# A convolution by transforms: real and imaginary parts on the two partition halves, and one full-height product per frequency

## The chip, the cores and the metric

The kernel runs on one core of a Trainium2 chip. The metric is device time in microseconds (us), the median of several runs. The core's engines are TensorE (PE in the profile; its weight loads are listed apart as PEld), VectorE (DVE), ScalarE (ACT), GpSimd (POOL) and SyncE (SP, which here only issues DMAs).

## What is computed

```python
def _attn_ref(x, h):                       # x (8, 5696, 128), h (5696, 128)
    B, S, D = x.shape
    L = 2 * S
    Xf = np.fft.rfft(x, n=L, axis=1)
    Hf = np.fft.rfft(h, n=L, axis=0)
    y = np.fft.irfft(Xf * Hf[None], n=L, axis=1)[:, :S, :]
    return y

def _moe_ref(x, w_theta, w_tok_r, w_tok_i, w_ch):
    theta = x @ w_theta
    zr, zi = x * np.cos(theta), x * np.sin(theta)
    y = np.einsum('ts,bsd->btd', w_tok_r, zr) + np.einsum('ts,bsd->btd', w_tok_i, zi)
    u = x + y
    return u + np.maximum(u @ w_ch, 0.0)
```

The second function gets what the first returns. The first is a long convolution over the sequence for every batch and channel; the second mixes tokens with two 5696 x 5696 matrices. The change lies wholly in the first.

## The kernel before

**The convolution** is done by transforms that are split in two factors: 5696 = 89 x 64 (N1 = NB = 89, N2 = 64), with K1 = 90 frequencies in the first factor. The work goes in eight groups. A group (L129) is two batch entries (called e = 0 and 1) and one half of the channels (HD = 64, called d). The transform of h is made once, ahead of the groups, by the same code. A group passes through these stages:

- **Stage A** (L245 to L263), 16 chunks of four d. For one d, the weights are x at [89 rows, 2 x 64 columns] (both batch entries, L477) and what streams is the table f1_t, 180 columns: 90 cosines and 90 sines. So one product (L255) puts 128 rows (e, n) and 180 columns (real and imaginary part, frequency) into PSUM. A chunk's four products are taken to the tile `a` by one copy of 128x720, on ACT (L262) or on DVE (L260).
- **f2** (L270 to L282), 12 chunks of up to eight frequencies. The tile `a` has the batch entry on its partition halves (64 rows each). For one frequency there are four products (L278) of 64 rows: two batch entries, and for each the real part and the imaginary part, which are added up in PSUM. The table `w_t2` holds 3 x 64 columns a frequency, so that a window of 128 columns gives either of the two; its lower and upper partitions hold the same frequencies, 45 slots apart (`slot`, L186). A chunk is copied to `xs` by ACT (L404, 128x1024), in the order e, d, frequency. For h, ACT takes batch entry 0's place (L332) and DVE the other (L333).
- **Products** with the transform of h, two for each chunk (L408, DVE).
- **Stage C** (L429, 16 chunks of 16 products) and **stage D** (L453, 7 chunks), with copies on ACT (L435, L459) or DVE (L433, L457).

All PSUM tiles of these stages come from one pool of four, each two banks wide (L100, L103).

**The order** is written out by hand. ACT and DVE (and, up to L507, POOL) keep program order. The string `PLAN` (L511) gives, for one group, the order of the chunks of stage C and D of a group (c, d), of stage A of the next one (a) and of its f2 and products (f, p, q, r); a capital letter puts the copy on DVE. `PLAN_0` is that of the first group, in which the e tables are made as well (t). When stage A of a group is through, POOL issues the loads of x for the next but one (L139), since x has a single buffer; they are 16 DMAs a group.

**The tables** are made at the start. For `w_t2`, three blocks of 15 slots: POOL writes indices (`index`, L157), DVE turns them into turns (`w_turns`, L191), ACT rounds them (L192), DVE takes the part below one and its absolute value (`w_angles`, L164 and L167), ACT takes the sines (`w_sines`, L170 and L173). `w_rest` (L205) completes a block on DVE: the odd half by a factor (L209), the negative third (L210), and two copies across the partition halves (L212) into the other 45 slots. The copy of h to its tile (L297) stands behind `w_rest(0)` on DVE; `w_rest(1)` and `w_rest(2)` stand ahead of and behind stage A of h. On POOL the first loads of x (L139, from L292) follow the indices.

**The token mixing** comes after all groups, from some 420 us on: products of 128x512 (L1299, L1387), whose weights are loaded by POOL's DMAs and transposed by DVE. One row of tiles in it (L1263) uses weights of 64 columns and writes the two halves of the PSUM partitions in turn.

Of the kernel before, what the change touches and what calls it, by code (L numbers as in the profile page):

```python
# [23 lines left out]
def kernel(  # L24
# [10 lines left out]
    nc = tc.nc  # L35
# [96 lines left out]
    def load_x(g):  # L132
# [11 lines left out]
    in_order = ExitStack()  # L144
    in_order.enter_context(tc.manual_schedule(engines={
        mybir.EngineType.DVE, mybir.EngineType.Activation, mybir.EngineType.Pool}))
    lane = fc.tile([P, 7], F32)
    for p0 in (0, 64):
        nc.gpsimd.iota(lane[p0:p0 + 64, 0:1], pattern=[[0, 1]], base=0, channel_multiplier=1,
                       allow_small_or_imprecise_dtypes=True)  # L150
    nc.gpsimd.iota(lane[:, 1:2], pattern=[[0, 1]], base=0, channel_multiplier=1,
                   allow_small_or_imprecise_dtypes=True)
    nc.vector.memset(lane[0:64, 2:3], QUARTER)
    nc.vector.memset(lane[64:P, 2:3], QUARTER + KH)

    def index(k, pattern, base):
        nc.gpsimd.iota(k, pattern=pattern, base=base, channel_multiplier=0,  # L157
                       allow_small_or_imprecise_dtypes=True)
# [10 lines left out]
    def sine(out_, r, sign):  # L169
        nc.scalar.activation(out_, r, AF.Sin, bias=zero_b[:r.shape[0]], scale=-sign * TWO_PI)  # L170

    def cosine(out_, k):
        nc.scalar.activation(out_, k, AF.Sin, bias=half_pi[:k.shape[0]], scale=-TWO_PI)  # L173

    w_t2 = keep.tile([P, K1, 3 * N2], F16, tag="keep", name="w_t2")
    assert WB + BT + 3 * P * 2 <= K1 * 3 * N2
    f1_t = fc.tile([P, 2 * K1], F16)
    odd = lane[:, 4:5]
    WS = 15
    WQ = WS * 32  # L180
    w_all = s1.tile([P, 2 * KH // WS * WQ], F32, name="w_all")
    w_of = [tuple(w_all[:, (2 * b + n) * WQ:(2 * b + n + 1) * WQ] for n in range(2)) for b in range(KH // WS)]
# [3 lines left out]
    def slot(e, k1):  # L186
        return (k1 + e * KH) % K1

    def w_turns(b):
        t, k = w_of[b]  # L190
        nc.vector.tensor_scalar(t, k, lane[:, 2:3], lane[:, 3:4], op0=add, op1=mult)  # L191
        nc.scalar.activation(k, t, AF.Identity, bias=magic)  # L192

    def w_angles(b):
        t, k = w_of[b]
        below_one(t, k)
        absolute(k, t)

    def w_sines(b):
        t3, k3 = (z.rearrange("p (k n) -> p k n", n=32) for z in w_of[b])  # L200
        here = w_t2[:, WS * b:WS * b + WS]
        sine(here[:, :, :32], t3, 1)
        cosine(here[:, :, N2:N2 + 32], k3)

    def w_rest(b):  # L205
        s0 = WS * b
        here = w_t2[:, s0:s0 + WS]
        two = here[:, :, :2 * N2].rearrange("p k (f a n) -> p k f a n", f=2, a=2)
        nc.vector.tensor_scalar(two[:, :, :, 1], two[:, :, :, 0], odd, None, op0=mult)  # L209
        nc.vector.tensor_scalar(here[:, :, 2 * N2:], here[:, :, :N2], -1.0, None, op0=mult)  # L210
        for p0 in (0, 64):
            nc.vector.tensor_copy(w_t2[p0:p0 + 64, KH + s0:KH + s0 + WS],  # L212
                                  w_t2[64 - p0:P - p0, s0:s0 + WS])

    nc.scalar.activation(f1_t[:, :1], zero_b, AF.Sin, bias=zero_b)
    for b in range(len(w_of)):
        index(w_of[b][1], [[1, WS], [N1, 32]], WS * b)
        if b == 0:
            index(f_k, [[1, K1]], 0)
# [5 lines left out]
    below_one(o_t, o_k)  # L225
    absolute(o_k, o_t)
    nc.vector.tensor_scalar(odd, o_k, -4.0, 1.0, op0=mult, op1=add)
    w_turns(0)
    nc.vector.tensor_scalar(f_t, f_k, QUARTER, lane[:NB, 5:6], op0=add, op1=mult)
    up(f_t, f_k)  # L230
    below_one(f_t, f_k)
    absolute(f_k, f_t)
    w_turns(1)
    w_angles(0)
    w_sines(0)
    sine(f1_t[:NB, K1:], f_t, -1)
    cosine(f1_t[:NB, :K1], f_k)
    w_turns(2)
    w_angles(1)
    w_sines(1)  # L240
    w_angles(2)
    w_sines(2)
    w_rest(0)

    def stage_a(lhs):  # L245

        st = {}

        def chunk(n, on_dve=False):
            q = 4 * n  # L250
            if q == 0:
                st["a"] = fa.tile([P, 2 * K1, HD], F16, tag="a", name="a_")
            ps = psum()
            for i in range(4):
                nc.tensor.matmul(ps[:, i // 2, (i % 2) * 2 * K1:(i % 2 + 1) * 2 * K1], lhs(q + i), f1_t[:NB],  # L255
                                 start=True, stop=True)
            a_out = st["a"][:, :, q:q + 4].rearrange("p k (a q) -> p k a q", a=2)
            a_in = ps[:, :, :4 * K1].rearrange("p a (q k) -> p k a q", q=2)
            if on_dve:
                nc.vector.tensor_copy(a_out, a_in)  # L260
            else:
                nc.scalar.activation(a_out, a_in, AF.Copy)  # L262
        return chunk, st  # L263

    def steps_of(chunk, count, on_dve=()):
        return [lambda n=n: chunk(n, n in on_dve) for n in range(count)]
# [3 lines left out]
    def f2(a_st, c):  # L270

        c0, ck = CHK[c]
        ps = psum()
        for j in range(ck):
            for ri in range(2):
                for e in range(2):
                    rows = slice(64 * e, 64 * e + 64)
                    nc.tensor.matmul(ps[:, e, j * HD:(j + 1) * HD],  # L278
                                     w_t2[rows, slot(e, c0 + j), N2 * (1 - ri):N2 * (3 - ri)],
                                     a_st["a"][rows, ri * K1 + c0 + j, :],  # L280
                                     start=(ri == 0), stop=(ri == 1))
        return ps[:, :, :ck * HD].rearrange("p e (k d) -> p e d k", k=ck)  # L282

    def woven(*lists):

# [13 lines left out]
    h_chunk_a, a_h = stage_a(lambda q: h16[:NB].rearrange("p h n d -> p (h n) d")[:, :, q])  # L299
    w_rest(1)  # L300
    for f in steps_of(h_chunk_a, NA, (4, 6, 8, 10, 12, 14)):
        f()
    w_rest(2)

    for t in uv_t:
        nc.gpsimd.memset(t[:, :, UVW:], 0.0)
# [15 lines left out]
    def h_part(c):  # L322
        return h_flat(c).rearrange("p (r d k) -> p r d k", r=2, k=CHK[c][1])
# [5 lines left out]
    def h_chunk(c):  # L329
        c0, ck = CHK[c]  # L330
        ps = f2(a_h, c)
        nc.scalar.activation(h_part(c)[:, 0], ps[:, 0], AF.Copy, scale=8.0 / S)  # L332
        nc.vector.tensor_scalar(h_later[:, HD * c0:HD * (c0 + ck)].rearrange("p (d k) -> p d k", k=ck),  # L333
                                ps[:, 1], 8.0 / S, None, op0=mult)

    def h_other(c, n):
        own = halves(hs_of[c][0], c, n, hs_of[c][1])
# [60 lines left out]
    def stage_b(a_st, refill):  # L398
        xs_of, made = {}, [0] * NCK

        def spectrum(c):
            ps = f2(a_st, c)
            xs = xs_of[c] = fs.tile([P, 2, HD, CK], F16, tag="xs", name="xs")
            nc.scalar.activation(xs[:, :, :, :CHK[c][1]], ps, AF.Copy)  # L404

        def products(c, e):
            c0, ck = CHK[c]
            nc.vector.tensor_tensor(  # L408
                uv[e][:, :, :, c0:c0 + ck],
                xs_of[c][:, e:e + 1, :, :ck].to_broadcast([P, 2, HD, ck]), h_part(c), op=mult)  # L410
# [62 lines left out]

    def front(g):
        dh = groups[g][1]
        x16 = x16s[g].rearrange("p b n d -> p (b n) d")
        chunk, a_st = stage_a(lambda q: x16[:NB, :, q])  # L477
# [223 lines left out]
    def load_ya1(yt=None):  # L701

        st = sides["phases"]
        if yt is None:
            a_ = fa.tile([P, 2 * K1, HD], F16, tag="a", name="ya1")
            ya = st[1] = a_.rearrange("p k d -> p (k d)")[:, :4 * H].bitcast(BF16).rearrange(
                "p (b t) -> p b t", b=4)
# [742 lines left out]
```

## Time and profile before

| What | us |
|---|---|
| Median of three runs | 2001.38 |
| Lowest and highest of them | 1993.42, 2003.62 |
| The profiled execution's own time | 2004.24 |
| Its span | 2002.4 |
| PE busy, whole span | 1931.3 |
| DVE, ACT, POOL busy, whole span | 1559.2, 647.2, 957.2 |
| L429 on PE, both kinds (2048 products) | 127.1 and 126.8 |
| L255 on PE, for x (512) | 52.7 |
| L408 on DVE (192) | 117.8 |
| L404 on ACT (96) | 88.4 |

A row of the timeline reads: start, length, engine, line, operation, what it writes and reads, shape, count, and in brackets how long the engine stood still before and what released it. "issue" as a releaser means that the profile shows nothing that the engine waited for. The ends of matmuls are modelled, so the spacing of their starts is the better measure. The granted clock (PEclk) is a share of full speed; where it reads 0.50, the same product takes twice as long to stream.

### The profile page before, as it was taken

The numbers are of one execution on the slowest core, as the hardware profiler recorded it, in microseconds if no ns is written. First come the engines' busy times: TensorE is split into PE (matmuls) and PEld (weight loads), VectorE is DVE, ScalarE is ACT, GpSimd is POOL, SyncE is SP. The second block draws the span as 40 slices with busy tenths as digits, with TensorE's granted clock in tenths as the row PEclk, the third lists the DMA queues.
The fourth block names the chain that finished last, engine by engine and source line by source line (L and its number), as shares of the span: only waits on it lengthen the run. The fifth ranks groups of instructions, "written<-read, shape, count | busy, mean of one in ns | idle before, by whom it ended". The sixth has DMA issues, their size and how long they took to land.

```text
span 2002.4 us, 41243 instructions
## 1 busy us (share of the span) xinstructions
PE 1931.3 (96%) x15757; PEld 1069.0 (53%) x15757; DVE 1559.2 (78%) x2897; ACT 647.2 (32%) x965; POOL 957.2 (48%) x1716
## 2 busy tenths in 40 slices
PE   5898998899999999999999999999999999999998
PEld 5798997554444444444444444444444444444444
DVE  8877778777888888888886778677786776867767
ACT  6898898831323232333310001011111111111112
POOL 8634223355446364554557555535445355454550
PEclk9899899999999999999999999999999999999999
DMA  9989778899989898898999899878869788697883
GB/s 112 71 95 146 85 117 202 231 230 191 168 178 178 173 174 170 159 185 173 182 167 153 146 272 213 129 131 149 149 121 157 134 146 150 125 154 136 142 153 85
DMA packets 490294, 312.02 MB, mean 156 GB/s; under 512 B 184471, under 2 KB 451607, under 8 KB 489111
## 3 DMA queue, kind: packets, MB, share of 16 engines
q0 software_dynamic: 320976, 153.46, 61.5%
q1 hardware_dynamic: 161952, 142.17, 24.3%
q10 hardware_dynamic: 7168, 13.76, 2.0%
q8 instruction: 123, 2.02, 0.4%
q14 instruction: 75, 0.61, 0.1%
HBM read 354.37 MB, written 90.29 MB: 222 GB/s over the span
## 4 chain that ended last, share of the span: by engine, by line
PE 72%; DMA 3%; DVE 2%; issue 1%; POOL 1%; ACT 0%; ACTq 0%; DVEq 0%; POOLq 0%
PE m L1387 64%; PE m L1299 3%; DMA b<-z_hbm 2%; PE v L1054 1%; PE utp L1047 1%; DVE c L1394 1%; PE m L1391 1%; PE m L1263 1%; POOL ring L661 1%; PE theta_ps L544 1%; PE tpz L995 1%; PE misc L1299 0%; DVE wt L967 0%; DMA c<-cp_hbm 0%; DMA ring<-in_moe_w_tok_i_dram 0%
## 5 line engine op out<-in xcount | busy, mean ns | idle before, releaser
L661 POOL DMA_DIRECT2D ring<-in_moe_w_tok_i_dram x720 | 388.1, 547 | 658.1 <-DVE wt L967 577.8
L661 POOL DMA_DIRECT2D ring<-in_moe_w_tok_r_dram x720 | 386.9, 547 | 120.9 <-DVE wt L967 73.3
L967 DVE STREAM_TRANSPOSE wt<-ring 128x384 f32<-128x384 f32 (+2 forms) x720 | 358.6, 523 | 101.7 <-PE m L1387 64.1
L1387 PE MATMUL m<-b,wt 128*128 128x512 bf16 x1640 | 388.3, 379 | 1.9 <-DVE wt L967 1.7
L1387 PEld LDWEIGHTS <-wt 128*128 128x128 bf16 x1804 | 176.1, 98 | 215.8 <-DVE wt L967 4.3
L1394 DVE TENSOR_TENSOR c<-c,m 128x512 f32<-128x512 f32 x412 | 265.3, 668 | 0.4 <-PE m L1387 0.4
L1049 ACT ACTIVATE ring<-utp 128x512 bf16<-128x512 bf16 x85 | 50.7, 597 | 575.9 <-PE utp L1047 575.9
L139 POOL DMA_DIRECT2D x<-in_x_dram x128 | 99.5, 797 | 129.1 <-PE ps L255 118.9
L429 PE MATMUL ps<-r_u,uv 128*128 128x128 f16 x1024 | 127.1, 223 | 11.0 <-issue 5.3
L429 PEld LDWEIGHTS <-uv 128*128 128x128 f16 x2048 | 122.2, 100 | 13.2 <-issue 6.5
L429 PE MATMUL ps<-r_v,uv 128*128 128x128 f16 x1024 | 126.8, 223 | 0.0
L408 DVE TENSOR_TENSOR uv<-xs,hs 128x1024 f16<-128x1024 f16 x192 | 117.8, 660 | 8.3 <-ACT xs L404 6.7
L1299 PE MATMUL m<-b,wt 128*128 128x512 bf16 x440 | 106.4, 379 | 3.7 <-DMA b<-zr_hbm 2.3
L1044 ACT ACTIVATE ub<-c 128x512 bf16<-128x512 f32 x88 | 55.1, 628 | 161.3 <-DVE c L1394 81.7
L404 ACT ACTIVATE xs<-ps 128x1024 f16<-128x1024 f32 x96 | 88.4, 991 | 9.0 <-PE ps L278 6.2
L1299 PEld LDWEIGHTS <-wt 128*128 128x128 bf16 x528 | 50.7, 98 | 62.5 <-issue 4.8
L546 ACT ACTIVATE red<-theta_ps,magic 128x512 f32<-128x512 f32 (+1 forms) x46 | 31.6, 687 | 128.6 <-PE theta_ps L544 100.5
L997 ACT ACTIVATE ring<-tpz 128x512 bf16<-128x512 bf16 (+1 forms) x46 | 27.4, 597 | 139.7 <-PE tpz L995 122.6
L278 PEld LDWEIGHTS <-w_t 64*128 64x128 f16 x3240 | 57.2, 100 | 15.3 <-issue 9.1
L875 DVE TENSOR_TENSOR b<-b 128x1024 bf16<-128x1024 bf16 x100 | 61.4, 682 | 4.3 <-DMA y_hbm<-b 4.2
L1056 DVE SCALAR_TENSOR_TENSOR c<-v,c 128x512 f32<-128x512 f32 x88 | 59.9, 682 | 2.6 <-PE v L1054 2.6
L566 ACT ACTIVATE mag<-red 128x512 f32<-128x512 f32 (+1 forms) x46 | 29.0, 631 | 94.6 <-DVE red L548 94.6
(2934 smaller groups left out, 3677.3 us busy)
## 6 DMA issues: line engine op xcount, KB each, us to landing
ring<-in_moe_w_tok_r_dram POOLq DMA_DIRECT2D x352, 96.0 KB, 4.6
ring<-in_moe_w_tok_i_dram POOLq DMA_DIRECT2D x352, 96.0 KB, 5.0
ring<-in_moe_w_tok_r_dram POOLq DMA_DIRECT2D x352, 80.0 KB, 4.5
ring<-in_moe_w_tok_i_dram POOLq DMA_DIRECT2D x352, 80.0 KB, 3.9
cp_hbm<-c SPq DMA_DIRECT2D x88, 256.0 KB, 2.5
c<-cp_hbm SPq DMA_DIRECT2D x88, 256.0 KB, 4.5
out_dram<-c SPq DMA_DIRECT2D x88, 256.0 KB, 4.4
yy<-y_hbm SPq DMA_DIRECT2D x84, 128.0 KB, 2.4
```

The lines of the kernel that those rows point to most:

```text
L139: nc.gpsimd.dma_start(x16[p0:p1, e, n0:n0 + 16, :HD], bass.AP(tensor=src.tensor, offset=src.offset + (p0 * N2 + n0) * D + dh * HD, ap=[[N2 ...
L278: nc.tensor.matmul(ps[:, e, j * HD:(j + 1) * HD], w_t2[rows, slot(e, c0 + j), N2 * (1 - ri):N2 * (3 - ri)], a_st["a"][rows, ri * K1 + c0 + ...
L404: nc.scalar.activation(xs[:, :, :, :CHK[c][1]], ps, AF.Copy)
L408: nc.vector.tensor_tensor(uv[e][:, :, :, c0:c0 + ck], xs_of[c][:, e:e + 1, :, :ck].to_broadcast([P, 2, HD, ck]), h_part(c), op=mult)
L429: nc.tensor.matmul(o, uv_t[e][:, r, d * K1:d * K1 + P], r_, start=(r == 0), stop=(r == 1))
L661: nc.gpsimd.dma_start(wb[32 * i:32 * i + 32, :ng, :nj * 64], bass.AP(tensor=a.tensor, offset=a.offset + row0 * S + p * H + i * QR + j0 * 6 ...
L875: return [lambda f=f, x=x: f(*x) for f, x in ((nc.vector.tensor_sub, (bt[M3], b12, b22)), (nc.vector.tensor_sub, (bt[M4], b21, b11)), (nc. ...
L967: nc.vector.transpose(wt.rearrange("p j t r -> p (j t r)").bitcast(F32).rearrange("p (j g t) -> p g j t", j=TJ, g=4)[:, :ng, :nj], wb[:, : ...
L1056: nc.vector.scalar_tensor_tensor(c[:m], v[:m], 0.0, c[:m], op0=ALU.max, op1=ALU.add)
L1299: ins = nc.tensor.matmul(ms[n // 2 * 2 + h], a[n][:, j, :, r], bts_of[p][jj][n % 2 * 2 + h][:, r, :], start=(n % 2 == 0 and jj == 0 and r ...
L1387: nc.tensor.matmul(ms[q], a[q][:, j, :, r], bts[jj][q][:, r, :], start=(jj == 0 and r == 0), stop=(jj == NJ - 1 and r == 1 and q not in left))
L1394: nc.vector.tensor_tensor(c, z, ms[q], op=op)
```

## The change

Stage A now makes four products for one d: for each batch entry, weights of [89, 64], once with the 90 cosines into PSUM partitions 0 to 63 and once with the 90 sines into partitions 64 to 127. So the tile `a` has the real part on its lower and the imaginary part on its upper partitions, and both batch entries beside each other in 128 columns. The copies of a chunk take as many elements as before, in another order.

In f2 one product per frequency follows: 128 rows (both parts), 128 columns of the table, 128 columns of `a`. The sum of the two parts is made inside the product, so nothing is added up in PSUM. The copies read eight frequencies 128 columns apart (`by_four`).

The table now holds 2 x 64 columns for each of the 90 frequencies, and its partition halves differ by a quarter turn (the new column 2 of `lane`). All six blocks of 15 are computed; the third that `w_t2` no longer needs serves as room for the angles. The turns of block 0 are made by DVE, those of the other five by POOL, from one index tile and six columns of `lane`. The negative third and the copies across the halves are gone. Two blocks' angles and sines (4 and 5) and two of the completions (2 and 3) are put between the chunks of stage A of h, and completions 4 and 5 behind it.

```diff
-    nc.vector.memset(lane[0:64, 2:3], QUARTER)
-    nc.vector.memset(lane[64:P, 2:3], QUARTER + KH)
+    nc.vector.memset(lane[0:64, 2:3], 0.0)
+    nc.vector.memset(lane[64:P, 2:3], -0.25)
...
     def w_turns(b):
         t, k = w_of[b]
-        nc.vector.tensor_scalar(t, k, lane[:, 2:3], lane[:, 3:4], op0=add, op1=mult)
+        (nc.gpsimd if b else nc.vector).tensor_scalar(t, w_k0, lane[:, 3:4], lane[:, 7 + b:8 + b], op0=mult, op1=add)
+
+    def w_round(b):
+        t, k = w_of[b]
         nc.scalar.activation(k, t, AF.Identity, bias=magic)
...
     def w_rest(b):
-        s0 = WS * b
-        here = w_t2[:, s0:s0 + WS]
-        two = here[:, :, :2 * N2].rearrange("p k (f a n) -> p k f a n", f=2, a=2)
+        two = w_t2[:, WS * b:WS * b + WS].rearrange("p k (f a n) -> p k f a n", f=2, a=2)
         nc.vector.tensor_scalar(two[:, :, :, 1], two[:, :, :, 0], odd, None, op0=mult)
-        nc.vector.tensor_scalar(here[:, :, 2 * N2:], here[:, :, :N2], -1.0, None, op0=mult)
-        for p0 in (0, 64):
-            nc.vector.tensor_copy(w_t2[p0:p0 + 64, KH + s0:KH + s0 + WS],
-                                  w_t2[64 - p0:P - p0, s0:s0 + WS])
...
+    for b in range(NW):
+        nc.vector.tensor_scalar(lane[:, 7 + b:8 + b], lane[:, 3:4], QUARTER + WS * b, lane[:, 2:3], op0=mult, op1=add)
     w_turns(0)
+    w_round(0)
...
-    w_turns(1)
+    for b in range(1, NW):
+        w_turns(b)
+    w_round(1)
     w_angles(0)
     w_sines(0)
     sine(f1_t[:NB, K1:], f_t, -1)
     cosine(f1_t[:NB, :K1], f_k)
-    w_turns(2)
-    w_angles(1)
-    w_sines(1)
-    w_angles(2)
-    w_sines(2)
+    for b in range(1, 4):
+        w_round(b + 1)
+        w_angles(b)
+        w_sines(b)
+    w_round(5)
     w_rest(0)
+    w_rest(1)
...
             for i in range(4):
-                nc.tensor.matmul(ps[:, i // 2, (i % 2) * 2 * K1:(i % 2 + 1) * 2 * K1], lhs(q + i), f1_t[:NB],
-                                 start=True, stop=True)
-            a_out = st["a"][:, :, q:q + 4].rearrange("p k (a q) -> p k a q", a=2)
-            a_in = ps[:, :, :4 * K1].rearrange("p a (q k) -> p k a q", q=2)
+                for e in range(2):
+                    for ri in range(2):
+                        nc.tensor.matmul(ps[64 * ri:64 * ri + 64, e, i * K1:(i + 1) * K1], lhs(e, q + i),
+                                         f1_t[:NB, ri * K1:(ri + 1) * K1], start=True, stop=True)
+            a_out = st["a"][:, :, :, q:q + 4]
+            a_in = ps[:, :, :4 * K1].rearrange("p e (q k) -> p k e q", q=4)
...
         for j in range(ck):
-            for ri in range(2):
-                for e in range(2):
-                    rows = slice(64 * e, 64 * e + 64)
-                    nc.tensor.matmul(ps[:, e, j * HD:(j + 1) * HD],
-                                     w_t2[rows, slot(e, c0 + j), N2 * (1 - ri):N2 * (3 - ri)],
-                                     a_st["a"][rows, ri * K1 + c0 + j, :],
-                                     start=(ri == 0), stop=(ri == 1))
-        return ps[:, :, :ck * HD].rearrange("p e (k d) -> p e d k", k=ck)
+            nc.tensor.matmul(ps[:, j // 4, j % 4 * D:(j % 4 + 1) * D], w_t2[:, c0 + j, :],
+                             a_st["a"][:, c0 + j].rearrange("p e d -> p (e d)"), start=True, stop=True)
+        nj = min(ck, 4)
+        return ps[:, :ck // nj, :nj * D].rearrange("p b (j x) -> p x b j", x=D)
+
+    def by_four(t):
+
+        return t.rearrange("p d (b j) -> p d b j", j=min(t.shape[2], 4))
...
-    w_rest(1)
-    for f in steps_of(h_chunk_a, NA, (4, 6, 8, 10, 12, 14)):
+    for n, f in enumerate(steps_of(h_chunk_a, NA, (4, 6, 8, 10, 12, 14))):
         f()
-    w_rest(2)
+        if n in (1, 5):
+            w_angles(4 + n // 4)
+            w_sines(4 + n // 4)
+        elif n in (3, 7):
+            w_rest(2 + n // 4)
+    w_rest(4)
+    w_rest(5)
...
-            nc.scalar.activation(xs[:, :, :, :CHK[c][1]], ps, AF.Copy)
+            nc.scalar.activation(by_four(xs.rearrange("p e d k -> p (e d) k")[:, :, :CHK[c][1]]), ps, AF.Copy)
```

More of the change, by code (lines that the diff above doesn't have):

```diff
@@ L146 @@
         mybir.EngineType.DVE, mybir.EngineType.Activation, mybir.EngineType.Pool}))
-    lane = fc.tile([P, 7], F32)
+    lane = fc.tile([P, 13], F32)
     for p0 in (0, 64):
@@ L173, in cosine @@
         nc.scalar.activation(out_, k, AF.Sin, bias=half_pi[:k.shape[0]], scale=-TWO_PI)
-    w_t2 = keep.tile([P, K1, 3 * N2], F16, tag="keep", name="w_t2")
+    w_t3 = keep.tile([P, K1 * 3 * N2], F16, tag="keep", name="w_t2")
+    w_t2 = w_t3[:, :K1 * 2 * N2].rearrange("p (k n) -> p k n", k=K1)
+    w_free = w_t3[:, K1 * 2 * N2:].bitcast(F32)
     assert WB + BT + 3 * P * 2 <= K1 * 3 * N2
@@ L180 @@
     WQ = WS * 32
-    w_all = s1.tile([P, 2 * KH // WS * WQ], F32, name="w_all")
-    w_of = [tuple(w_all[:, (2 * b + n) * WQ:(2 * b + n + 1) * WQ] for n in range(2)) for b in range(KH // WS)]
+    NW = K1 // WS
+    w_all = s1.tile([P, (NW + 1) * WQ], F32, name="w_all")
+    w_k0 = w_all[:, :WQ]
+    w_of = [(w_all[:, (1 + b) * WQ:(2 + b) * WQ], w_free[:, b * WQ:(b + 1) * WQ]) for b in range(NW)]
     f_t, f_k = (z[:NB, :K1] for z in (s1.tile([P, K1], F32, name="f_t"), s1.tile([P, K1], F32, name="f_k")))
     o_t, o_k = s1.tile([P, 1], F32, name="o_t"), s1.tile([P, 1], F32, name="o_k")
-    def slot(e, k1):
-        return (k1 + e * KH) % K1
     def w_turns(b):
         t, k = w_of[b]
-        nc.vector.tensor_scalar(t, k, lane[:, 2:3], lane[:, 3:4], op0=add, op1=mult)
+        (nc.gpsimd if b else nc.vector).tensor_scalar(t, w_k0, lane[:, 3:4], lane[:, 7 + b:8 + b], op0=mult, op1=add)
+    def w_round(b):
+        t, k = w_of[b]
         nc.scalar.activation(k, t, AF.Identity, bias=magic)
@@ L201, in w_sines @@
         here = w_t2[:, WS * b:WS * b + WS]
-        sine(here[:, :, :32], t3, 1)
-        cosine(here[:, :, N2:N2 + 32], k3)
+        cosine(here[:, :, :32], k3)
+        sine(here[:, :, N2:N2 + 32], t3, -1)
     def w_rest(b):
-        s0 = WS * b
-        here = w_t2[:, s0:s0 + WS]
-        two = here[:, :, :2 * N2].rearrange("p k (f a n) -> p k f a n", f=2, a=2)
+        two = w_t2[:, WS * b:WS * b + WS].rearrange("p k (f a n) -> p k f a n", f=2, a=2)
         nc.vector.tensor_scalar(two[:, :, :, 1], two[:, :, :, 0], odd, None, op0=mult)
-        nc.vector.tensor_scalar(here[:, :, 2 * N2:], here[:, :, :N2], -1.0, None, op0=mult)
-        for p0 in (0, 64):
-            nc.vector.tensor_copy(w_t2[p0:p0 + 64, KH + s0:KH + s0 + WS],
-                                  w_t2[64 - p0:P - p0, s0:s0 + WS])
     nc.scalar.activation(f1_t[:, :1], zero_b, AF.Sin, bias=zero_b)
[L216 to L219, printed above, removed]
+    index(w_k0, [[1, WS], [N1, 32]], 0)
+    index(f_k, [[1, K1]], 0)
     nc.vector.tensor_scalar(lane[:, 3:4], lane[:, 0:1], 1.0 / S, None, op0=mult)
@@ L251, in chunk @@
             if q == 0:
-                st["a"] = fa.tile([P, 2 * K1, HD], F16, tag="a", name="a_")
+                st["a"] = fa.tile([P, K1, 2, HD], F16, tag="a", name="a_")
             ps = psum()
             for i in range(4):
-                nc.tensor.matmul(ps[:, i // 2, (i % 2) * 2 * K1:(i % 2 + 1) * 2 * K1], lhs(q + i), f1_t[:NB],
-                                 start=True, stop=True)
-            a_out = st["a"][:, :, q:q + 4].rearrange("p k (a q) -> p k a q", a=2)
-            a_in = ps[:, :, :4 * K1].rearrange("p a (q k) -> p k a q", q=2)
+                for e in range(2):
[4 more added lines that the diff above has]
+            a_in = ps[:, :, :4 * K1].rearrange("p e (q k) -> p k e q", q=4)
             if on_dve:
@@ L298 @@
                               raw_h[:NB, :N2 * D].rearrange("p (n h d) -> p h n d", h=2, d=HD)[:, :, :, d0:d0 + 32])
-    h_chunk_a, a_h = stage_a(lambda q: h16[:NB].rearrange("p h n d -> p (h n) d")[:, :, q])
-    w_rest(1)
-    for f in steps_of(h_chunk_a, NA, (4, 6, 8, 10, 12, 14)):
-        f()
-    w_rest(2)
+    h_chunk_a, a_h = stage_a(lambda e, q: h16[:NB, e, :, q])
+    for n, f in enumerate(steps_of(h_chunk_a, NA, (4, 6, 8, 10, 12, 14))):
+        f()
+        if n in (1, 5):
[5 more added lines that the diff above has]
+    w_rest(5)
     for t in uv_t:
@@ L331, in h_chunk @@
         ps = f2(a_h, c)
-        nc.scalar.activation(h_part(c)[:, 0], ps[:, 0], AF.Copy, scale=8.0 / S)
-        nc.vector.tensor_scalar(h_later[:, HD * c0:HD * (c0 + ck)].rearrange("p (d k) -> p d k", k=ck),
-                                ps[:, 1], 8.0 / S, None, op0=mult)
+        nc.scalar.activation(by_four(h_part(c)[:, 0]), ps[:, :HD], AF.Copy, scale=8.0 / S)
+        nc.vector.tensor_scalar(by_four(h_later[:, HD * c0:HD * (c0 + ck)].rearrange("p (d k) -> p d k", k=ck)),
+                                ps[:, HD:], 8.0 / S, None, op0=mult)
     def h_other(c, n):
@@ L475, in front @@
         dh = groups[g][1]
-        x16 = x16s[g].rearrange("p b n d -> p (b n) d")
-        chunk, a_st = stage_a(lambda q: x16[:NB, :, q])
+        x16 = x16s[g]
+        chunk, a_st = stage_a(lambda e, q: x16[:NB, e, :, q])
         return chunk, stage_b(a_st, dh == 0 and groups[g + 1][1] == 1)
@@ L704, in load_ya1 @@
         if yt is None:
-            a_ = fa.tile([P, 2 * K1, HD], F16, tag="a", name="ya1")
-            ya = st[1] = a_.rearrange("p k d -> p (k d)")[:, :4 * H].bitcast(BF16).rearrange(
+            a_ = fa.tile([P, K1, 2, HD], F16, tag="a", name="ya1")
+            ya = st[1] = a_.rearrange("p k e d -> p (k e d)")[:, :4 * H].bitcast(BF16).rearrange(
                 "p (b t) -> p b t", b=4)
```

## Prediction

> **What bounds the kernel now.** I read the page's chain of work first, then its 40 slices, then a table by stretches, then the timeline and the idle times of TensorE in the first 360 us.
>
> ```profile
> PE 72%; DMA 3%; DVE 2%; issue 1%; POOL 1%; ACT 0%; ACTq 0%; DVEq 0%; POOLq 0%
> ```
>
> The chain runs on TensorE, most of it in L1387: the token mixing from about 420 us to the end, which the change doesn't touch. So what the change does to the first 360 us moves the end by as much, and nothing else does. There, eight groups follow each other; the first f2 product (L278) of each starts at 44.9, 76.9, 111.1, 147.4, 181.5, 219.3, 258.9 and 291.4 us. A group has two stretches: a/c (stage A of the next group and half of stage C) and f/d (frequencies, the other half of C, and D). Columns below: stretch, its length, busy time of PE, PEld, DVE, ACT, POOL, granted clock, DMA share, GB/s.
>
> ```profile
> core 0: us, PE busy (x) PEld busy (x) DVE busy (x) ACT busy (x) POOL busy (x), PEclk, DMA share, GB/s
> ...
> 147.00:169.00 22.00, 20.19 (x628) 19.02 (x626) 17.16 (x24) 19.88 (x23) 11.44 (x16) 1.00 1.29 127
> 169.00:181.00 12.00, 11.81 (x186) 11.69 (x185) 9.93 (x14) 11.94 (x17) 0.94 (x2) 1.00 0.70 175
> 181.00:207.00 26.00, 20.70 (x629) 19.28 (x627) 16.80 (x24) 20.11 (x24) 11.03 (x15) 1.00 1.20 102
> ...
> 243.00:258.70 15.70, 15.70 (x202) 15.70 (x200) 9.84 (x14) 12.97 (x17) 1.23 (x2) 0.78 0.41 94
> 258.70:279.00 20.30, 19.90 (x623) 18.83 (x621) 16.73 (x24) 19.63 (x23) 10.72 (x15) 1.00 1.19 76
> 279.00:291.00 12.00, 11.93 (x187) 11.83 (x187) 10.00 (x14) 11.88 (x17) 1.01 (x2) 1.00 0.54 124
> ```
>
> An a/c stretch takes 12.0 us at the full clock, and both PE and ACT are full in it. An f/d stretch takes 20.3 us when nothing disturbs it (258.7 on), with ACT full and TensorE with some slack; others take 22 to 26 us with the same work. What fills them is TensorE standing still for no reason that the profile names:
>
> ```profile
> 185.42 0.22 PE L429 MATMUL ps<-r_u,uv 128*128 128x128 f16 x1 [2.05 <-issue]
> 193.26 0.22 PE L429 MATMUL ps<-r_u,uv 128*128 128x128 f16 x1 [2.96 <-issue]
> ```
>
> Such pauses sum to 1.6, 1.8, 5.3 and 1.8 us in the f/d stretches from 111, 147, 181 and 219 us, which are 4.2, 1.7, 5.7 and 3.7 us over 20.3. Two of them also fall to half clock (mean 0.86), and so does the a/c stretch from 243 us (15.7 for 12.0).
>
> **The change, part by part. Rates first.** At full clock:
>
> ```profile
> 228.76 1.62 PE L278 MATMUL ps<-a__5257,w_t 64*128 64x64 f16 x96
> ...
> 230.32 1.02 PE L453 MATMUL ps<-e_t,g__5283 89*128 89x89 f16 x20
> ```
>
> 96 half-height products take 1.55 us until the next kind starts: 16.1 ns each, 65 ns for the four of a frequency. The new product (128x128 weights, 128 columns) has the shape of L429, which starts every 56 ns (226.04 to 226.94 us: 16). At half clock it is 30 x 4 = 121 (32 in 0.97 us at 237.75) against 107 ns. So f2 drops by 9 ns x 90 = 0.8 us a group.
>
> Stage A now takes 77.5 ns for one d (8 in 0.62 us: L255 starts at 250.27, L429 at 250.90). It becomes four products of 90 columns into the two column halves. The trace has such products only in L1263, with 512 columns:
>
> ```profile
> 1141.13 1.03 PE L1387 MATMUL m<-b,out__17310 128*128 128x512 bf16 x4
> 1142.09 0.40 PE L1263 MATMUL m<-ring,out__17393 128*64 128x512 bf16 x1
> 1142.10 0.62 PE L1263 MATMUL m<-ring,wt 128*64 128x512 bf16 x2
> ```
> ```profile
> 1145.98 0.11 PEld L1263 LDWEIGHTS <-out__17451 128*64 128x64 bf16 x1 [1.09 <-DVE out__17451 L976]
> 1145.99 0.14 PEld L1263 LDWEIGHTS <-wt 128*64 128x64 bf16 x2
> 1146.02 0.32 PEld L1263 LDWEIGHTS <-out__17451 128*64 128x64 bf16 x2
> ```
>
> The two halves start within 10 ns of each other, a pair every 216 ns: they run side by side. Four weight loads start within 40 ns. So a pair of 90 columns costs its stream, 37.5 ns (90 of 180 columns at half of 75), plus 2.7 ns (216 less 512 columns) to 5.4 ns (an f2 pair, 32.2 less 26.7): 40 to 43, and one d 80 to 86 ns. That is +0.2 to +0.5 us a group. At half clock it is 150 both ways. Entering the other shape costs: four L1387 at 0.216 from 1141.13 end at 1141.99, L1263 starts at 1142.09, so 0.10 us; f2 loses 0.09 on entry today (228.61 + 0.056 to 228.76), and 0.0 to 0.1 on leaving. From L255 to L429 nothing is lost now. The plan string has 7 runs of a in a group, so 7 x 0.13 to 0.2 = 0.9 to 1.4 us move into the a/c stretch, and as much leaves f/d with its 7 runs of f.
>
> **In a/c** TensorE is full (16 x 0.31 + 8 x 0.90 = 12.2 us), so the stretch grows by 1.1 to 1.9 us; ACT, which trails it by some 0.7 us, hides part. I take +1.2 x 7 stretches = **+8.4** (ends 0 and +14). Group 0 and h do stage A alone and are paced by evictions or the half clock. **In f/d** TensorE's savings (0.8 us and the switches) lie beside ACT: **0** (ends -5 and 0).
>
> **Evictions** move the same element counts. The new reading order of L404 (eight values 512 B apart) is that of L435, 1.02 us against L404's 1.03; L262 and L260 keep 720 elements (0.77, 0.91). I take 0; if the order cost 5% of ACT's 31 us, it would be +1.5 a group, which I hold unlikely.
>
> **The pauses.** They come in the f/d stretches, in or just after the load of x (POOL's L139). TensorE's own stream there is 628 products, each with a weight load; the change takes 270 products out of it and puts 192 into a/c, where DMA is at 0.54 to 0.70 instead of 1.2. If TensorE waits for its instructions, the pauses shrink. All of them with the half clock behind them are 4.2 + 1.7 + 5.7 + 3.7 + 3.7 = 19.0 us; I take six tenths, nearer to the row without a pause because the stream loses 43% there: **-11** (ends -19 and 0). [...] No view names the cause of a pause.
>
> Group 0 has one of 4.1 us at 54.27, but DVE's products (L408) set its pace and stood still only 0.8 us: **-0.8** (ends -4 and 0).
>
> **The start.** h has landed at 12.5 us (second issue at 2.29, 10.2 to land); DVE's copy L297 starts at 14.56, behind the tables. DVE loses two L191 (0.5 each) and, of w_rest(0), L210 and L212 (2.2); it gains six one-column operations (0.4), one more block of angles (1.06) and a second L209 (0.5 to 0.8). But angles(3) wait for ACT's tenth piece: from 5.6 us, nine of 0.59 and two short ones give 11.7; then 1.06 and two L209 bring the copy to about 14.0, so -0.5. Behind that wait on DVE only L209 and the copy stand. POOL's five new operations (0.56 for 356 elements in L379, so some 0.7 each) move the x loads from 5.2 to 8.4 us; all were in at 25, x is first read at 35.8, so 3 us later costs nothing; the cover is 10 us. L295's loads and POOL's e tables come 1 to 3 us later, before 41. Stage A of h runs at 152 ns a d, the pace that 243.6 us shows at a granted 0.50 (149), though the clock reads 1.00 there; ACT gets four sines more (2.4 us) in its 9.8 us, of which ACT's evictions fill 7.7: +0.6. Then DVE has two L209 (1.2) in place of 3.2 us before its first L333 (29.57); but TensorE gives a chunk only each 0.86 us there: -0.4 to -2. I take **-1.2** for the whole start (ends -4 and +4).
>
> **Sum:** 8.4 - 11 - 0.8 - 1.2 = -4.6. The profiled execution took 2004.24 us (span 2002.4 and 1.84 around it), so 1999.6; the median of the runs shown is 2.86 below it: **1997 us**.
>
> **Rivals.**
> 1. *The pauses go whole and the switches hide under ACT.* Then 2 - 19 - 0.8 - 1.2 = -19, **1982**. For it: the excess follows the pauses nearly one to one (5.7 for 5.3). Against: PE is full in a/c.
> 2. *The weight loads of the two halves don't overlap* (slower). A load of 128 strided columns (L255, 148 ns against 98 packed) fits into 77.5 ns, so 64 columns take up to 39, and those of one half start 30 to 40 ns apart above: four in a row are 128 to 155 for 77.5. It decides as soon as a pair of loads outlasts the 43 ns of its stream. At the low end 50 x 64 = 3.2 us and 1.1 for switches, x 7 = +30; h's stage at half clock +4 (four loads of twice 26.7 for 150, x 64); with -11, -0.8 and -1.2: +21, **2022**. Against: the four loads within 40 ns. [...]
> 3. *The pauses stay*, since they follow DMA and not the stream: 8.4 - 1.2 - 0.8 = +6.4, **2008**. For it: the 4.1 us pause fell where DMA was at 1.5 to 1.7.
>
> That the products don't become fewer is excluded by the loops: 360 + 64 become 90 + 256.
>
> **Chances.** Forecast 0.49 (own range 1988 to 2006), rival 1 0.20, rival 2 0.15, rival 3 0.16. About 10 us, 0.5%, is what a measurement of this kernel can tell from no change. Faster by more: rival 1 and a fifth of the forecast, 0.29; slower by more: rival 2 and a third of rival 3, 0.20; between, 0.51. The range leaves out half of rival 1 and two thirds of rival 2: 1982 to 2018.
>
> **What will show it.** a/c stretches of 13 to 14 us with 0.1 us between runs (right), of 16 or more (rival 2); d every 80 to 86 ns; f2 every 56; f/d near 20.3 with hardly an issue pause (right), or 22 to 26 as now (rival 3); L297 at about 14.0. I am wrong altogether if ACT's evictions change their length, or if the granted clock in a/c falls.

## The result, and the profile after

The changed kernel takes **2115.82 us** (median of four runs, 2112.36 to 2121.52), the one before 1997.4 beside it: a ratio of 1.0605 with an interval of 1.0577 to 1.0632. It is slower by 6%, where the prediction had 1997 and a range up to 2018. The profiled execution took 2117.79 us, its span is 2116.0, and its mean granted clock is 0.952.

Lines of the page of the changed kernel: its chain of work, its clock by slices and three groups of instructions (busy time, mean ns of one, idle time before them). L438 is stage C (L429 before), L259 stage A (L255 before), L279 f2:

```profile
PE 66%; DMA 3%; DVE 3%; issue 1%; POOL 1%; ACT 0%; ACTq 0%; SPq 0%; DVEq 0%; POOLq 0%
...
PEclk9677777999999999999999999999999999999999
...
L438 PE MATMUL ps<-r_u,uv 128*128 128x128 f16 x1024 | 157.8, 251 | 6.6 <-DVE uv L417 4.9
...
L259 PE MATMUL ps<-f_t,x 89*64 89x90 f16 x2048 | 141.6, 325 | 4.5 <-DVE g__1169 L442 0.9
L259 PEld LDWEIGHTS <-x 89*64 89x64 f16 x2048 | 133.1, 220 | 13.9 <-issue 12.6
```

The second to seventh of the 40 slices (a slice is 53 us) stand at a clock of 0.6 to 0.7. That is the convolution, and everything lies there: the last f2 product of the last group starts at 426.0 us (before: 309.8), and what follows takes 1690 us against 1693. The busy time of stage C, which the change doesn't touch, went from 127.1 to 157.8 us for one of its two kinds of product and from 126.8 to 158.4 for the other.

The stretches of two groups, in the columns of the table that the prediction shows (f/d, a/c, f/d, a/c):

```profile
core 0: us, PE busy (x) PEld busy (x) DVE busy (x) ACT busy (x) POOL busy (x), PEclk, DMA share, GB/s
208.30:229.00 20.70, 19.34 (x356) 18.62 (x354) 17.68 (x26) 19.23 (x22) 9.59 (x13) 0.99 1.32 132
229.00:259.80 30.80, 30.67 (x378) 28.76 (x378) 9.08 (x13) 13.81 (x16) 2.56 (x4) 0.51 0.45 105
259.80:281.00 21.20, 19.64 (x358) 18.85 (x356) 18.00 (x26) 19.26 (x23) 9.47 (x13) 1.00 1.07 68
281.00:311.00 30.00, 29.99 (x373) 28.22 (x374) 8.77 (x11) 13.49 (x16) 2.23 (x3) 0.54 0.24 52
```

The f/d stretches came out as forecast, 20.7 and 21.2 us, and quiet: from 44 us on, in the eight groups, TensorE stands still without a named reason for 0.2 us in all, against 14.9 before. The a/c stretch takes 30 to 31 us in place of 12.0. TensorE hardly stands still in it (30.67 of 30.80 us busy), ACT and DVE have become idle for over half of it, and the clock reads 0.51 and 0.54. In the last group, where the stretch from 383 to 408 us has a clock of 0.93, it takes 25 us. The timeline of the changed kernel shows how slowly stage A's products come:

```profile
16.12 16.18 PE L259 MATMUL ps<-f_t,h 89*64 89x90 f16 x256 [16.12 <-DVE h L301]
...
41.98 15.93 PE L259 MATMUL ps<-f_t,x 89*64 89x90 f16 x254 [0.25 <-issue]
...
202.94 2.21 PE L259 MATMUL ps<-f_t,x 89*64 89x90 f16 x32
...
208.34 1.06 PE L279 MATMUL ps<-a__2989,w_t 128*128 128x128 f16 x16
```

The length of such a row less the last product (0.33 us at half clock, 0.22 at full), over the count less one, is the mean spacing of starts: 62 ns for h, 62 for the first group, 61 between stage C's runs. In the last group, at full clock, it is 61 too (32 in 2.19 us, where one lasts 0.30). Four of them are some 250 ns for one d; the wide product took 77.5. f2 is at the forecast 56 ns (0.84 us over 15).

The products of the two column halves, and their weight loads, start in pairs. These rows have two of each in the length of one:

```profile
395.31 0.20 PEld L259 LDWEIGHTS <-x 89*64 89x64 f16 x2
395.31 0.32 PE L259 MATMUL ps<-f_t,x 89*64 89x90 f16 x2
```

So 62 ns is a mean: a pair comes every 121 to 125 ns.

### The profile page after: what moved, and what is told of

It reads as the page before. It is cut to its first block, busy times and chain, and to the rows that moved or that the text cites. A ratio compares the mean times of both kernels' runs of the same rounds, so it can differ in the third digit from the quotient of the medians.

```text
span 2116.0 us, 39711 instructions
## 1 busy us (share of the span) xinstructions
PE 2041.8 (96%) x14879; PEld 1182.2 (56%) x15055; DVE 1556.8 (74%) x2901; ACT 661.0 (31%) x974; POOL 957.5 (45%) x1719
## 4 chain that ended last, share of the span: by engine, by line
PE 66%; DMA 3%; DVE 3%; issue 1%; POOL 1%; ACT 0%; ACTq 0%; SPq 0%; DVEq 0%; POOLq 0%
PE m L1396 59%; PE m L1308 3%; DMA b<-z_hbm 2%; DVE c L1403 1%; PE v L1063 1%; PE utp L1056 1%; POOL ring L670 1%; PE m L1400 1%; PE m L1272 1%; DVE wt L976 1%; DMA ring<-in_moe_w_tok_i_dram 1%; PE misc L1308 0%; PE tpz L1004 0%; PE theta_ps L553 0%; DMA b<-zz 0%
## 5 line engine op out<-in xcount | busy, mean ns | idle before, releaser
L438 PE MATMUL ps<-r_u,uv 128*128 128x128 f16 x1024 | 157.8, 251 | 6.6 <-DVE uv L417 4.9
L438 PE MATMUL ps<-r_v,uv 128*128 128x128 f16 x1024 | 158.4, 252 | 0.0
L438 PEld LDWEIGHTS <-uv 128*128 128x128 f16 x2048 | 149.2, 115 | 11.4 <-DVE uv L417 5.2
L259 PE MATMUL ps<-f_t,x 89*64 89x90 f16 x2048 | 141.6, 325 | 4.5 <-DVE g__1169 L442 0.9
L259 PEld LDWEIGHTS <-x 89*64 89x64 f16 x2048 | 133.1, 220 | 13.9 <-issue 12.6
```

The costliest lines, as they stand in the source:

```text
L259: nc.tensor.matmul(ps[64 * ri:64 * ri + 64, e, i * K1:(i + 1) * K1], lhs(e, q + i), f1_t[:NB, ri * K1:(ri + 1) * K1], start=True, stop=True)
L438: nc.tensor.matmul(o, uv_t[e][:, r, d * K1:d * K1 + P], r_, start=(r == 0), stop=(r == 1))
```

## The experiments

Every one is compared with the kernel before, run on the same chip. They start from the theory (L below) that the four weight loads of a d queue one after another (rival 2 in the prediction, with 62 ns a load in place of 32 to 39), and had to find whether that, the stream, the clock or the order of the halves sets the 62 ns. e2, e3, e4, e6 and e7 were run once each. Runs of the kernel before on one chip differ by up to 18 us (1990.95 to 2009.19), so of these five only large differences and the rows of their profiles count.

**e1_wide_a: the old stage A alone put back.**

```diff
-                for e in range(2):
-                    for ri in range(2):
-                        nc.tensor.matmul(ps[64 * ri:64 * ri + 64, e, i * K1:(i + 1) * K1], lhs(e, q + i), ...)
+                nc.tensor.matmul(ps[:, i // 2, (i % 2) * 2 * K1:(i % 2 + 1) * 2 * K1], lhs(q + i), f1_t[:NB], ...)
```

> Stage A's products as before (one of 128 columns of weights and 180 streamed columns per d), the rest as changed; so the tile a gets the batch entries on its halves, while f2 takes them for the two parts, and the output is not the reference's. Theory L (the weight loads of column halves, some 62 ns each, one after another, make stage A's cost): the a/c stretches fall back from 25 to 31 us to about 12, the whole to 1975 to 2005 us. Rival F (the full-height f2, the new copies' order or the tables cost it): it stays over 2060.

Measured: 1979.22 us, ratio 0.9921 (0.9904 to 0.9938). All the rest of the change (tables, start, full-height f2) is worth a gain of 16 us, and the whole loss comes with stage A's new products. The f2 products of three groups in a row (columns: shortest, median and longest ns, first and last start in us):

```profile
L277 PE MATMUL ps<-a__1523,w_t x90: 217/219/220, 109.2 to 126.5; 128*128 128x128 f16 x90
L277 PE MATMUL ps<-a__2221,w_t x90: 216/219/220, 141.2 to 158.5; 128*128 128x128 f16 x90
L277 PE MATMUL ps<-a__2943,w_t x90: 216/219/220, 173.2 to 190.5; 128*128 128x128 f16 x90
```

From there on the groups are 32.0 us apart to the tenth, with no pause at all; before they were 32.0 to 39.6.

**e2_full_width: four products a d as in the change, but with all 128 weight columns** (`ps[:, e, ...]` and the wide `lhs`), so no column halves.

> As changed, but each of the four products of a d uses all 128 columns of weights (both batch entries) and writes all 128 partitions, so the two parts overwrite each other and the output is not the reference's. As many products, loads and streamed columns as in the changed kernel, without column halves. Theory L: the products start every 40 ns at full clock, a/c takes about 17.5 us, the whole 2030 to 2050. Rival N (four small products and loads in place of one, whatever their width): the spacing stays at 60 to 63 ns and the whole at 2100 to 2125.

Measured: 2078.17 us, between the two ranges. The spacing that theory L gave (40 ns) was missed:

```profile
16.14 23.28 PE L259 MATMUL ps<-f_t,h 89*128 89x90 f16 x256 [16.14 <-DVE h L301]
...
49.00 16.36 PE L259 MATMUL ps<-f_t,x 89*128 89x90 f16 x256 [0.33 <-DVE h L342]
```

63 ns for x, the mean of the change. But here a load fills the full width with 128 columns every 63 ns, and in the change each half gets one of 64 columns every 125 ns. For h it is 90, where the elements are 128 B apart instead of 136, and where a mean product lasts 299 ns for x's 238, with a clock that reads 1.00 (before, one of h lasts 356 ns at a reading of 1.00, where one of x lasts 241 and, at 0.50, 356 to 359). A halved clock alone doesn't make the 90: e5 below has x's first 128 products at a granted 0.50 and 75 ns apart, which is their stream. (Streams are estimates here and below, from the 150 ns that 180 columns of L255 take before at a granted 0.50, eight from 247.70 to 248.90 us: 75 ns for 90 columns, 107 for 128, and half of it at 1.00.) The clock was at 1.00 in the a/c stretches, but for 6.8 us in each of two, so the price of the loads alone can be read against e1: +99 us, of which h's products are 12 (23.3 us for 11.1), and 87 remain for eight groups. That is 10.9 each; 64 d of 250 less 77.5 ns give 11.0.

**e3_stream_128: the change with 128 streamed columns for 90** (38 of no use; `f1_t` padded with zeros, the reads of PSUM cut to 90).

> As changed, but each product of stage A streams 128 columns in place of 90 (the 38 more are computed and not used). Theory L: the spacing stays at 60 to 65 ns since the stream was not the limit, the whole 2105 to 2130. [...] Rival C (streams this short let the clock fall, and the clock is the cost): the a/c stretches show a granted clock near 1.00 and the whole falls to about 2070.

Measured: 2087.44 us, 28 less than the change (26 when each is taken against the kernel before on its chip), for 42% more streaming; that lies between the values of L and C. A timeline row and the stretch from 200 to 250 us:

```profile
41.62 16.38 PE L260 MATMUL ps<-f_t,x 89*64 89x128 f16 x256 [0.33 <-DVE h L343]
```
```profile
200.00:250.00 50.00, 48.28 (x798) 46.39 (x796) 29.18 (x40) 36.62 (x43) 15.95 (x22) 0.93 0.99 130
```

The spacing is the same 63 ns, and 62 at a granted 0.50 (from 128 us) as at 1.00, so the stream (107 and 53 ns) doesn't set it; the clock between 200 and 250 us is 0.93, against 0.70 for the change in the same 50 us. So I put the 28 us down to the clock: stage C and D, which are woven in, run faster by it (stage C's products start every 107 ns at 0.50 and every 56 at 1.00 in the change, from 201.74 and from 391.26 us).

**e4_by_half: the order ri, e, i**, so 8 products follow each other in one column half.

```diff
-            for i in range(4):
-                for e in range(2):
-                    for ri in range(2):
+            for ri in range(2):
+                for e in range(2):
+                    for i in range(4):
```

> As changed, but the sixteen products of a chunk are ordered by column half: eight for the lower partitions, then eight for the upper ones. Theory L (one path for the loads of both halves): the spacing stays at 60 to 65 ns and the whole at 2105 to 2130. [...]

Measured: 2154.63 us, 25 over theory L's range, with a mean of 67 ns in the first group and 79 between stage C's runs:

```profile
42.29 17.33 PE L259 MATMUL ps<-f_t,x 89*64 89x90 f16 x256 [0.33 <-DVE h L342]
...
201.21 2.79 PE L259 MATMUL ps<-f_t,x 89*64 89x90 f16 x32
...
203.29 0.70 PE L259 MATMUL ps<-f_t,x 89*64 89x90 f16 x4
```

The last row is the end of the run of 32: four products of the upper half, with no other load beside them. They start 123 ns apart (0.70 less 0.33 us, over 3). So one strided load into one half takes 123 ns with nothing to queue behind, and theory L (62 ns each, one after another) is wrong. Where the order lets both halves work, products of both run side by side, each half at 123 to 125 ns; in the change's order this is so throughout, and the mean of 62 is half of it. The runs of eight leave one half alone at the start and the end of each 32 products, which gives the 79 here and less of it in the first group's 256. Nor is the 123 a sum of load and stream: the change has 121 to 122 ns a pair between stage C's runs with 37.5 as with 75 ns of stream, and e3 123 to 124 with 53 as with 107.

**e5_split_90: the kernel before, with each wide product cut into two of 90 columns**, the weights loaded twice.

> The kernel before, but each product of stage A is cut into two of 90 streamed columns with the same 128 columns of weights, so the weights are loaded twice a d. Theory L2 (every load of these strided weights takes TensorE 62 to 64 ns, of 64 or of 128 columns, and they queue): a d takes 126 ns in place of 77.5, the spacing is 63, an a/c stretch at full clock 15 us for 12, the whole 2010 to 2025. Rival C2 (streams of 90 columns let the clock fall by themselves): a/c stretches at half clock throughout, the whole 2045 or more. Rival W (only the column halves are dear): a d takes 80 ns, the whole 1990 to 2003.

Measured: 2022.93 us, ratio 1.0119 (1.0069 to 1.0168), as L2 had it.

```profile
151.40 1.16 PE L257 MATMUL ps<-f_t,x 89*128 89x90 f16 x16
```

Also 63 ns a product (128 strided columns), here in the old kernel, without column halves, new order or new tables. Before, the load was hidden behind 180 streamed columns, at 77.5 ns a product.

**e6_packed_h: h laid out [half, d, n]**, so that stage A of h loads 64 elements that lie side by side; x as in the change.

> As changed, but the tile of h has n next to each other, so that the weights of h's stage A are 64 packed values in place of 64 values 128 B apart; x is left as it is. In the changed kernel h's 256 products take 16.1 us, 62.9 ns each. If the stride makes the load slow, the spacing falls to 40 ns or less at full clock (75 / 2 = 38 to 40 also at half) and stage A of h to about 10 us, the whole by 6. If the load of a column half takes that long whatever its stride, it stays at 16 us.

Measured: 2113.79 us. Stage A of h:

```profile
18.55 3.81 PE L259 MATMUL ps<-f_t,h 89*64 89x90 f16 x96 [18.55 <-DVE h L301]
24.36 6.59 PE L259 MATMUL ps<-f_t,h 89*64 89x90 f16 x160 [2.01 <-DVE a__195 L264]
```

37 and 39 ns for 62. That is the stream of two halves side by side at a halved clock (75 for two), the pace that h has before too (152 ns for 180 columns), though the clock reads 1.00 in both. The copy of h, now strided itself, took 3.65 us for 1.25 to 1.5, twice, and took most of it back: stage A of h ends 1.4 us earlier, and the whole is 2 us less, where 6 were expected. With the same column halves, elements that lie side by side cost no more than their stream, 37 to 39 ns for the 62 of those 128 B apart: what differs is the distance of the weight elements.

**e10_packed_all: the same for x and h, without a copy.**

```diff
-    h_chunk_a, a_h = stage_a(lambda e, q: h16[:NB, e, :, q])
+    h_chunk_a, a_h = stage_a(lambda e, q: h16[:NB, e, q, :])
-        chunk, a_st = stage_a(lambda e, q: x16[:NB, e, :, q])
+        chunk, a_st = stage_a(lambda e, q: x16[:NB, e, q, :HD])
```

> The changed kernel, but each weight load of stage A reads 64 elements that lie next to each other in a row of x or of h, in place of 64 elements 136 or 128 B apart. Same number, shape and place of products, loads, copies and transfers; what is left out is the right choice of elements (the transform runs over channels in place of the second factor), so the output is not the reference's. Theory (the stride of the load holds TensorE 62 ns, and the half-filled stream behind it lowers the clock): a pair then costs its stream, 40 to 43 ns, so one product every 20 to 22 ns and one d 80 to 86 in place of 250; the clock stays at 0.97 or above in the a/c stretches; 1979 of the run with the wide product plus 8 x 0.3 and 8 x 1.1 for the switches: 1985 to 2000. Rival T (the two column halves queue their loads whatever the stride): one product every 55 to 62 ns and 2090 to 2120. Rival H (stride mends the load, but products on half the columns count as half activity): 37 to 38 ns a product at a granted 0.50, one d 150, 4.6 us more a group for stage A and about 4 for stage C at half clock: 2040 to 2070.

Measured: 2006.69 us, ratio 1.0079 (1.0055 to 1.0102): of the change's 6.05% over the kernel before, 0.79% is left. The products are as the theory had them. The clock is too in four of six a/c stretches (1.00), not in the other two (0.91). The time is 7 us over its range. The timeline, a whole a/c stretch, and a pause:

```profile
135.20 0.83 PE L259 MATMUL ps<-f_t,x 89*64 89x90 f16 x32
135.97 0.23 PE L438 MATMUL ps<-r_u,uv 128*128 128x128 f16 x1
...
136.82 0.22 PE L438 MATMUL ps<-r_v,uv 128*128 128x128 f16 x1
136.97 0.83 PE L259 MATMUL ps<-f_t,x 89*64 89x90 f16 x32
...
143.22 0.68 PE L259 MATMUL ps<-f_t,x 89*64 89x90 f16 x25 [2.38 <-issue]
```
```profile
170.00:184.40 14.40, 14.20 (x392) 12.96 (x389) 10.32 (x15) 13.30 (x18) 1.39 (x2) 1.00 0.73 177
```

32 products take 0.83 less 0.21 us: 20 ns each, 80 for one d. From stage C's last product to stage A's first pass 0.15 us, 0.09 over its usual step, and 0.13 more on the way back (135.97 less 135.20, less 32 x 20). One run of 8 d with its 16 products of stage C takes 1.76 us (before: 1.52). T (55 to 62 ns) and H (half clock) fall. What the theory left out are the pauses: from 44 us on 8.5 us ahead of L259 and 2.3 ahead of L279 (once, just after an a/c stretch), that is, now mostly in the a/c stretches.

**e7_f2_half: the change, but f2 in four half-height products** as before.

> As changed, but f2 makes four half-height products per frequency again (weights w_t2 of either partition half, one batch entry's place each), copied in the old order; stage A with column halves and the new tables stay. The tile a has the parts on its halves, so the output is not the reference's. If stage A alone costs the time and the full-height f2 gives some 16 us back (as the run with stage A's old products has it, 1979), this comes to 2125 to 2140; if f2 and stage A together make the loss, it falls well below 2100.

Measured: 2124.16 us, 8 over the change and 1 under the expected range; pauses of 5.3 us are back. For a single run 8 us are within what runs of one kernel differ by.

**e8_f2_quarters: e1 with each f2 product cut into four of 32 columns**, to put as many products back into f/d without the old shapes.

> As the run with stage A's old products (output not the reference's for the same reason), but each full-height f2 product is cut into four of 32 streamed columns, so that f2 again has 360 products and loads a group. Theory P (the gain of f2 comes from the shorter stream of instructions in the f/d stretches, whose pauses go): the pauses come back and the whole goes to 1990 to 2000 us. Rival: the gain comes from f2's shape (no switch, no half-height pairs) or from the tables, and it stays at 1975 to 1985.

Measured: 2001.06 us, ratio 1.0006 (0.9986 to 1.0027), 22 over e1 (17 when each is taken against the kernel before on its chip) and 1 over the range of theory P, with 7.6 us of pauses.

```profile
113.82 1.75 PE L279 MATMUL ps<-a__2333,w_t 128*128 128x32 f16 x64
```

A frequency costs 100 ns here (25 a product: 1.75 less 0.18 us, over 63), for 56; and groups without a pause are 34.2 to 34.7 us apart, for 32.0 in e1. So the loss is of both kinds, and the run doesn't tell them apart, though its time is near what the theory of the pauses gave. It shows one thing more: 128 packed columns were loaded every 25 ns.

**e9_no_x_loads: the kernel before, without the loads of x for groups 2 to 7.**

> The kernel before, with the loads of x for groups 2 to 7 left out (they use group 1's x, so the output is not the reference's). Theory P (in the f/d stretches TensorE waits for its instructions, which come behind the descriptors of the x loads): the pauses without a named cause go and the whole comes to 1978 to 1988 us, as with the full-height f2. Rival: the pauses come from the order of the work or from f2's shape, stay, and the whole stays within 5 us of the kernel before; what the loads hold up otherwise is at most 1 to 2 us, since TensorE waits for none of them.

Measured: 1989.44 us, ratio 0.9972 (0.9954 to 0.9990), above the 1978 to 1988 of theory P and 5.0 us under the kernel before beside it, the rival's limit. Pauses of 6.5 us stay, one of them with no load of x under way:

```profile
179.34 0.22 PE L432 MATMUL ps<-r_u,uv 128*128 128x128 f16 x1 [2.15 <-issue]
```

So the loads of x aren't the sole cause of the pauses; that they lengthen them (14.9 us of pauses with them) rests on one profile of each kernel.

**What TensorE waits for in the pauses** can be read from the packets of DMA queue q8 in these traces. The pages of the kernel before and of e1 have (packets, MB, share):

```profile
q8 instruction: 123, 2.02, 0.4%
...
q8 instruction: 104, 1.70, 0.4%
```

The packets are of 16 KB. e1 has 2430 products fewer, each with its weight load, and 19 packets fewer: 4860 over 19 is 256 instructions of TensorE a packet, or 128 products with their loads (an estimate). In the groups from 44 us on, all twelve traces together have 34 pauses of over 0.35 us without a named releaser, and each of them ends 1.2 to 1.8 us after such a packet has landed. The pause of 4.11 us before 54.27 is one: its packet starts at 51.91, inside the pause, and has landed at 52.85. From this I read that in the pauses TensorE waits for its own instructions. At 31 products a us a packet lasts 4.1 us, at 17 some 7.5 (estimates from 128 products). Why a packet starts late isn't shown.

## Why the prediction was wrong, point by point

**Rates, stage A: the step that failed.** The prediction took a pair of 90-column products to cost its stream, 40 to 43 ns, and one d 80 to 86. It was some 125 and 250. It drew this from L1263, whose weight elements lie next but one to each other and which streams 512 columns behind each load, and it took L255's load of strided columns, which fitted into 77.5 ns, to shrink with the columns (39 ns for 64). Neither carries over. The two halves do run side by side, as it said, but a load of 64 elements 128 to 136 B apart takes 123 ns in its half (e4, alone there), at a clock of 0.50 and of 1.00 alike (the change, e3), and the pair comes at that pace. It isn't shorter than L255's load of 128 columns but longer: over the full width 128 such columns took 63 ns (e2, e5). With weights side by side (e10) the same four products took 80 ns, within the forecast 80 to 86. So the term was right for a layout that this kernel doesn't have. (Its 75 and 26.7 ns and the 512 columns that it takes from 216 are the stream at 150 ns for 180 columns at a granted 0.50, as above, halved.) Price: 11.0 us a group, 88 for eight, and 5 for h (16.2 us of stage A for e1's 11.1).

Taken together, 64 strided columns in a half took 123 ns, 128 over the full width 63, and packed ones at most 40 for 64 (a pair every 40 ns, e10) and 25 for 128 (e8). So the number of columns alone doesn't give the time of a load here: the distance of the elements counts, and the place in a half.

**Rival 2 had the right place and not the mechanism.** It let the loads of the two halves follow each other, four in 128 to 155 ns, with 2022 us and a chance of 0.15. They don't: e4's rows have 123 ns for one half alone, and the change has pairs. Its condition, that a pair of loads outlasts the 43 ns of its stream, held all the same, by the length of the single load. With the 250 ns measured it would have come to 64 x 172 ns x 7 = 77 us for the 50 ns x 64 x 7 = 22 that it counted. No run shows the load of 26.7 ns, 53 at half clock, that its +4 for h counts; e4 has 123. That the theory L of the experiments gave the right mean of 62 ns is luck: 123 in each of two halves looks like 62 in a queue.

**The granted clock in a/c**, which the prediction named as what would make it wrong altogether, and did not price: 0.51 and 0.54 in the stretches shown. It falls at 228.6 us, at the end of an f/d stretch with a stand-still of some 0.3 us, and comes back only with the next f/d. I read it as a consequence of the first fault: the same number of loads with 128 streamed columns (e3) has 0.93, with full-height products (e2) 1.00 in most stretches, with packed loads (e10) likewise. In the change each half streams 37.5 of 125 ns (counted at full clock). The price is some 28 us by e3 (26 chip by chip), which doesn't quite restore it; the 5 to 6 us between the a/c stretches at half clock, of which there are five, and that of the last group at 0.93 come to as much. Over the first of these stretches TensorE counts as busy for 30.67 of 30.80 us and stays at half clock. What sets the granted clock isn't in a trace; that it follows how much is streamed is my reading of these three runs. It can't be the whole rule: from 389 us on the change's last a/c stretch has the same products at the same spacing with the clock at 1.00.

**In a/c, switches**: forecast 0.13 to 0.2 us a run; e10 has 0.22, and its undisturbed a/c stretch is 14.4 us for the forecast 13 to 14. So the stretch grows by 2.4 us where the sum took 1.2: the right kind, at half its size.

**In f/d and evictions, 0**: right. f/d 20.7 and 21.2, copies as long as before.

**The pauses, -11**: the sign holds in the change, where they went whole (14.9 to 0.2 us), and in e1, which gains 16 us. In f/d they went for the reason that the prediction gave as an if: TensorE waits for its instructions, as I read it from the packets of q8 (each pause ends 1.2 to 1.8 us after one has landed), and with 270 products fewer a packet lasts longer (some 7.5 us for 4.1, the estimates above). What it had not counted is a/c: there the 192 products more kept clear of pauses in the change because they follow each other slowly. Where they run at speed (e10), 10.8 us of pauses are back, 8.5 of them in a/c, though the DMA share there is 0.35 to 0.73 instead of 1.2. So the pauses go with the stream of products: they came at 31 products a us (f/d before) and 27 (a/c of e10), and did not at 12 to 19 (e1, the change). It also means that without the slow loads the change would still have lost: e10 is 14 us over the kernel before beside it, where rival 3, in which the pauses stay, had +6.4.

**Group 0, -0.8**: in e1 its first f2 product and that of group 1 are 30.2 us apart, before 32.1 (with the pause of 4.1): -1.9, over twice the forecast. **The start, -1.2**: nothing. e1's first product of h starts at 16.14 us and of x at 36.16, before 16.12 and 36.24. The copy of h started at 14.86, not at the forecast 14.0 (before 14.56).

**The sum by the runs**: -16 (e1) + 88 and 5 for the loads + 10 for switches (some 1.2 to 1.4 x 7 or 8) + 28 for the clock = +115; measured +118. The switches are an estimate from e10 and the clock's term rests on a single run, so agreement to 3 us is in part luck.

## What to carry to other kernels

Before one product with much behind its weight load is cut into several, measure the load by itself, with its real distance of elements and in its real place (a column half or the full width): a load that is hidden shows only that it is shorter than what hides it (here 63 ns behind 77.5). Read single starts and not only their mean: here 62 ns looked like a queue and was two loads of 123 side by side. Here the loads were longer than their own stream, 123 ns for 37.5 in each half, and the clock of the stages that are woven in stood at 0.51 and 0.54 with it; with packed loads, a pair every 40 ns, it was at 0.90 to 1.00 (e10), and even so the whole was 0.79% over the kernel before. Look also at how many products a stretch issues per microsecond: with 270 fewer a group where they were densest (e1), 14.9 us of pauses went, in which, as I read q8, TensorE had waited for instructions.

## What was not expected of the hardware

- A weight load of 64 elements 136 B apart into a column half took 123 ns, alone (e4) or beside one into the other half, at a clock of 0.50 and of 1.00; one of 128 such columns over the full width took 63 (e2, e5), and 128 packed columns were loaded every 25 ns (e8). With 64 packed columns a half a product passed every 20 ns (e10).
- TensorE stayed at a granted clock of 0.50 for up to 31 us without standing still, where each column half streamed 37.5 of 125 ns (counted at full clock).
- Pauses of up to 4 us without a named reason came with 27 or more products a us and moved with them from one stage to another (e10); with 16 to 19 a us they were gone (e1). All 34 of over 0.35 us ended 1.2 to 1.8 us after 16 KB of instructions had landed.
